# Attention with two feed-forward layers on one Trainium2 core: probabilities transposed in place for one more batch, a shared ring of five buffers, and deeper loads of 64-bit weights

## The chip, the core and the metric

The kernel runs on one core of a Trainium2 chip. The metric is the device time of one execution in microseconds (us). The core's engines are named as the profile names them: PE is TensorE's matmul, PEld its weight load, DVE is VectorE, ACT is ScalarE, POOL is GpSimd, and SP is SyncE, which here issues nearly all DMA transfers. Each engine takes the instructions of its own queue in order.

## The reference

Attention over 4 batches, 12 heads, 448 positions and 64 values per head, then two feed-forward layers, all in float32:

```python
def rmsnorm(x, g):
    rms = np.sqrt(np.mean(x * x, axis=-1, keepdims=True) + 1e-06)
    return x / rms * g
q_n, k_n = (rmsnorm(q, g_q), rmsnorm(k, g_k))
scores = scale * np.matmul(q_n, k_n.transpose(0, 1, 3, 2))
scores = scores - np.max(scores, axis=-1, keepdims=True)
attn = np.exp(scores)
attn = attn / (np.sum(attn, axis=-1, keepdims=True) + 1e-09)
...
return np.matmul(attn, v).astype(np.float32)
...
x = np.ascontiguousarray(attn_out.transpose(0, 2, 1, 3)).reshape(B * S, H * D)   # 1792 x 768
...
h = x @ w_in                    # first layer, 768 -> 2048
r = np.maximum(h, 0.0)
g = r * r
return (g @ w_out).astype(np.float32)
...
a = x @ w1                      # second layer, 768 -> 1024 -> 1024 -> 768
b = x @ w2
h = a * b @ w3
return (h @ w_out).astype(np.float32)
```

The weights reach the kernel as 64-bit floats; q, k, v and the result are float32.

## The kernel before, in words

**Precision.** A float32 operand is split into a high part, which the matmul's fp32r type holds, and the remaining low part. Each product is then three fp32r matmuls (lines L262, L263, L264 in `mm3`): high by high, high by low, low by high.

**Weights.** They come in units of 128 rows by 384 or 512 values. A 64-bit unit is loaded into a `raw64` tile (the trace calls it `raw`, L180, on SP's queue). ACT rewrites its upper words (L194), POOL or ACT its lower ones (L200, L198), and DVE joins the two into a float32 tile `raw` (L207). ACT copies that to the high half of `hl` (L106), and POOL or DVE subtracts to get the low half (L114). For the weights of the first feed-forward layer and of `w1` and `w2` the joined unit is also stored to DRAM (L215), so that later batches load 32-bit units (L183). The function `advance` keeps these steps ahead of the matmuls: when unit i is split, loads are issued up to unit i + `LOAD64_AHEAD`, words are rewritten up to i + 3 and joined up to i + 2. With 4 `raw64` buffers the load of unit i + 5 goes into the buffer of unit i + 1.

**The order of the work.** A loop runs over the 48 heads (12 for each batch). In the iteration of head h, PE computes the scores of head h in two halves (`stage_qk`), ACT takes the exponential of each half into a tile `p` (`stage_exp`, L543), and PE transposes the probabilities of head h - 1 (`stage_t`, L570: four blocks of 128 or 64 columns, four transposes each, so 16 for a head) and multiplies them by v (`stage_v`, L622). Between these steps `fill` puts feed-forward matmuls into PE's queue. While the heads of batch 1 run, the matmuls are those of w3 times w_out (`gen_w3o`, with 32 64-bit units); while the heads of batch 2 run, they are the feed-forward layers of batch 1 (`gen_moe(0)`, with 88 64-bit units and their stores); while those of batches 3 and 4 run, the layers of batches 2 and 3, from 32-bit units. The layers of batch 4 come last, without attention beside them. The framework fixes the order of each engine's queue when the program is built, from this program order and its own estimates of when things are ready; the trace shows, for example, transposes set between the two score matmuls of a head.

**Transposing probabilities.** In the first batch PE transposes the float32 tile `p` itself, against a float32 identity. From the second batch on (`h >= H`, H is 12) each half head's `p` is first copied by a DMA on SP's queue (L549, 392 KB) into a tile `pw`, which is declared as fp32r. PE then transposes `pw` against an fp32r identity. `p` and `pw` have 3 buffers each:

```python
pp = t3.tile([P, 2, S], F32, name="p", tag="p")
...
if h >= H:
    words = t3.tile([P, 2, S], F32R, name="pw", tag="pw")
    nc.sync.dma_start(out=words.bitcast(F32), in_=pp)
    d["p"][c0:c0 + 2] = [words[:, 0, :], words[:, 1, :]]
```

In `stage_t` the transposed block is rounded to its high half by ACT (L106, `ptr`) and its low half is made by DVE (L114, `ptr`), with two PSUM buffers `pt`.

Of the kernel before, what the change touches and what calls it, by code (L numbers as in the profile page):

```python
# [8 lines left out]
F32 = mybir.dt.float32  # L9
F32R = mybir.dt.float32r  # L10
U16 = mybir.dt.uint16
U32 = mybir.dt.uint32
# [17 lines left out]
def attention_moe_kernel(  # L30
# [16 lines left out]
    B, P, H, C, D = q_nat.shape  # L47
    S = P * C
# [26 lines left out]
    JOIN_AHEAD = 2  # L75
    WORD_AHEAD = 3
    LOAD32_AHEAD = 3
    LOAD64_AHEAD = 5

    const = ctx.enter_context(tc.tile_pool(name="const", bufs=1))  # L80
    xp = ctx.enter_context(tc.tile_pool(name="x", bufs=8))
# [7 lines left out]
    t3 = ctx.enter_context(tc.tile_pool(name="t3", bufs=3))  # L89
# [9 lines left out]
    ident = const.tile([P, P], F32, name="ident")  # L99
    ident_r = const.tile([P, P], F32R, name="ident_r")  # L100
# [3 lines left out]
    def copy_on(eng, out, in_):  # L104
        if eng == "a":
            nc.scalar.activation(out=out, in_=in_, func=AF.Copy)  # L106
        elif eng == "g":
            nc.gpsimd.tensor_scalar(out=out, in0=in_, scalar1=1.0, scalar2=1.0, op0=ALU.mult, op1=ALU.mult)
        else:
            nc.vector.tensor_copy(out=out, in_=in_)  # L110
# [60 lines left out]
    def is64(i):  # L171
        return units[i][0].dtype != F32

    def load_next():
        i = pos["load"]
        src = units[i][0]
        n = src.shape[-1]
        if is64(i):
            t = t3.tile([128, 512, 2], U32, name="raw64", tag="raw64", bufs=4)
            nc.sync.dma_start(out=t[:, :n, :], in_=src.bitcast(U32).rearrange("p (n t) -> p n t", t=2))  # L180
        else:
            t = rawp.tile([128, 512], F32, name="raw", tag="raw")
            nc.sync.dma_start(out=t[:, :n], in_=src)  # L183
        raws[i] = t
        pos["load"] += 1

    def load_to(i):
        while pos["load"] <= min(i, NU - 1) and is64(pos["load"]):
            load_next()
# [50 lines left out]
    def advance(u):  # L240
        while pos["lo"] <= min(u + SPLIT_AHEAD, NU - 1):
            i = pos["lo"]
            for k in range(pos["load"], min(i + LOAD64_AHEAD, NU - 1) + 1):
                if is64(k):
                    load_next()
                elif k <= i + LOAD32_AHEAD and (k <= pos["join"] or not is64(k - 1)):
                    load_next()
                else:
                    break
            upto("store", min(i + JOIN_AHEAD, pos["join"]) - 1, lambda k: is64(k) and store(k))  # L250
            upto("word", i + WORD_AHEAD, lambda k: is64(k) and words(k))
            upto("join", i + JOIN_AHEAD, lambda k: is64(k) and join(k))
            upto("hi", i + HI_AHEAD, split_hi)
            upto("lo", i, split_lo)
# [274 lines left out]
    def stage_exp(h, s):  # L529
        if not (0 <= h < NH):  # L530
            return
        d = heads[h]
        nb, o = d.pop("nb"), d.pop("sc")
        i = h % 2
        if s == 0 and i == 0:
            sums2[h // 2] = small.tile([P, 2, C], F32, name="sm", tag="sm")
        sm = sums2[h // 2]
        c0 = 2 * s
        pp = t3.tile([P, 2, S], F32, name="p", tag="p")
        for j in range(2):  # L540
            c = c0 + j
            p = d["p"][c] = pp[:, j, :]
            nc.scalar.activation(  # L543
                out=p, in_=o[j], func=AF.Exp, scale=d["rq"][:, c:c + 1], bias=nb[:, j:j + 1],
                accum_out=sm[:, i, c:c + 1],
            )
        if h >= H:
            words = t3.tile([P, 2, S], F32R, name="pw", tag="pw")
            nc.sync.dma_start(out=words.bitcast(F32), in_=pp)  # L549
            d["p"][c0:c0 + 2] = [words[:, 0, :], words[:, 1, :]]  # L550
        if s == 1 and i == 1:
            nc.vector.tensor_scalar(out=sm, in0=sm, scalar1=1e-9, scalar2=None, op0=ALU.add)
            rs = small.tile([P, 2, C], F32, name="rs", tag="rs")
            nc.vector.reciprocal(out=rs, in_=sm)
            wide = t1.tile([P, C, 2, D], F32, name="rsw", tag="rsw")
            nc.gpsimd.tensor_scalar(
                out=wide, in0=rs.rearrange("p i c -> p c i").unsqueeze(3).to_broadcast([P, C, 2, D]),
                scalar1=1.0, scalar2=1.0, op0=ALU.mult, op1=ALU.mult,
            )
            sums2[h // 2] = wide.rearrange("p c i d -> p c (i d)")  # L560

    def stage_t(h, kc):
        if not (0 <= h < NH):
            return
        d = heads[h]
        k0, kn = KCS[kc]
        ps = ps_pt.tile([128, 512], F32, name="pt", tag="pt")
        to, one = (ps.bitcast(F32R), ident_r) if h >= H else (ps, ident)
        for c in range(C):
            nc.tensor.transpose(to[:kn, c * P:(c + 1) * P], d["p"][c][:, k0:k0 + kn], one)  # L570
        if kn == 128:
            t = t3.tile([128, 2, S], F32R, name="ptr", tag="ptr", bufs=3)
            hi, lo = t[:, 0, :], t[:, 1, :]
            d["pt"][kc] = [hi, lo]
        else:
            t = t1.tile([128, S], F32R, name="pte", tag="pte")
            hi, lo = t[:kn, :], t[kn:, :]
            d["pt"][kc] = [t]
        copy_on("a", hi, ps[:kn, :S])
        d["lo"].append((lo, ps[:kn, :S], hi.bitcast(F32)))  # L580
# [95 lines left out]
    for h in range(NH + 1):  # L676
# [5 lines left out]
        stage_qk(h, 0)  # L682
        fill(n)
        stage_exp(h, 0)
        if h % H != 1:
            stage_x(h - 2)
        stage_t(h - 1, 0)
        stage_t(h - 1, 1)
        fill(n)
        stage_lo(h - 1)  # L690
        if h < NH:
            v_prep(h)
        fill(n)
        stage_k(h + 1)
        stage_t(h - 1, 2)
        stage_t(h - 1, 3)
        fill(n)
        stage_lo(h - 1)
        stage_qk(h, 1)
        fill(n)  # L700
        stage_exp(h, 1)
        fill(n)
        stage_v(h - 1)
# [64 lines left out]
```

## Time and profile before

| | us |
|---|---|
| median of three runs | 1239.81 |
| lowest, highest | 1237.89, 1242.05 |
| the profiled execution, its own time | 1239.56 |
| its span in the trace | 1237.8 |

The profiled execution is 0.25 us under the median. Its span is 1.76 us shorter than its own time; that remainder lies around the instructions. In the span the first exponential of head 12 (batch 2) starts at 183.4, that of head 24 at 475.0 and that of head 36 at 749.0. The last probability transposes are at 1019, and from about 1030 on only feed-forward matmuls run. A matmul's busy time overlaps that of its neighbour, so the distance between two starts, not the time of one, says how fast PE goes.

### The profile page before, as it was taken

How to read it: one execution, taken by the hardware profiler on the slowest of the kernel's cores; microseconds unless marked ns; L12 is line 12 of the kernel's file. 1: busy time of each engine (PE TensorE's matmuls, PEld its weight loads, DVE VectorE, ACT ScalarE, POOL GpSimd, SP SyncE). 2: the span in 40 equal slices, each digit the busy share in tenths (PEclk: the TensorE clock that was granted, in tenths of full speed). 3: DMA queues.
4: the chain of work that ended last, by engine and by line, in shares of the span. 5: the costliest groups of instructions: out<-in, count | busy, mean ns of one | idle time of the engine just before them, and what ended most of it. 6: DMA issues, size and time to landing. Idle time of an engine off the chain costs nothing.

```text
span 1237.8 us, 18914 instructions
## 1 busy us (share of the span) xinstructions
PE 1166.3 (94%) x6192; PEld 1054.4 (85%) x6192; DVE 710.7 (57%) x1314; ACT 727.7 (59%) x1553; POOL 784.9 (63%) x772
## 2 busy tenths in 40 slices
PE   3799999898898999999999999999999999999998
PEld 1588887787787888998998998999999999999998
DVE  6699888878888685546567555655664421012110
ACT  5888867667746655655645655656545554443342
POOL 5875434565776756765776664756766556678673
PEclk9899999999999999999999999999999999999999
DMA  6774547787888866455445455454444443433342
GB/s 214 242 227 131 159 140 218 254 272 249 280 259 257 257 192 194 132 155 147 148 127 154 140 155 161 143 154 121 141 138 120 135 136 112 113 109 105 105 120 93
DMA packets 111347, 207.63 MB, mean 168 GB/s; under 512 B 12208, under 2 KB 66704, under 8 KB 111248
## 3 DMA queue, kind: packets, MB, share of 16 engines
q1 hardware_dynamic: 107792, 200.92, 53.8%
q10 hardware_dynamic: 3456, 5.51, 1.2%
q8 instruction: 49, 0.80, 0.3%
q14 instruction: 50, 0.41, 0.1%
HBM read 149.95 MB, written 27.53 MB: 143 GB/s over the span
## 4 chain that ended last, share of the span: by engine, by line
PE 59%; DMA 4%; DVE 4%; ACT 2%; POOL 1%; issue 1%; ACTq 0%; SPq 0%; POOLq 0%; DVEq 0%
PE mm L262 17%; PE mm L264 17%; PE mm L263 17%; PE kv L622 3%; PE pt L570 2%; DMA pw<-p 2%; PE sc L525 1%; PE sc L524 1%; DMA raw<-w 1%; POOL hl L114 1%; ACT p L543 1%; DMA kn<-k_nat 1%; PE kv L508 1%; DVE nb L526 1%; DVE raw L207 0%
## 5 line engine op out<-in xcount | busy, mean ns | idle before, releaser
L114 POOL TENSOR_TENSOR hl<-raw,hl 128x384 fp32r<-128x384 f32 (+1 forms) x383 | 447.0, 1171 | 254.5 <-ACT hl L106 250.9
L106 ACT ACTIVATE hl<-raw 128x384 fp32r<-128x384 f32 (+1 forms) x416 | 233.8, 564 | 146.8 <-PE mm L264 82.0
L262 PE MATMUL mm<-x,hl 128*128 128x448 f32 (+1 forms) x832 | 311.3, 374 | 4.4 <-ACT x L106 1.8
L263 PE MATMUL mm<-x,hl 128*128 128x448 f32 (+1 forms) x832 | 307.2, 369 | 8.1 <-POOL x L114 8.1
L264 PE MATMUL mm<-x,hl 128*128 128x448 f32 (+1 forms) x832 | 306.4, 368 | 3.7 <-DVE hl L114 3.3
L262 PE MATMUL mm<-act,hl 128*128 128x448 f32 (+1 forms) x640 | 238.3, 372 | 0.0
L263 PE MATMUL mm<-act,hl 128*128 128x448 f32 (+1 forms) x640 | 235.7, 368 | 2.3 <-POOL act L114 2.3
L264 PE MATMUL mm<-act,hl 128*128 128x448 f32 (+1 forms) x640 | 235.0, 367 | 0.6 <-POOL hl L114 0.6
L543 ACT ACTIVATE p<-sc,nb,rr 112x448 f32<-112x448 f32 x192 | 137.4, 720 | 82.4 <-DVE nb L527 82.0
L263 PEld LDWEIGHTS mm<-x,hl 128*128 128x128 f32 x832 | 158.5, 190 | 21.9 <-POOL x L114 9.7
L262 PEld LDWEIGHTS mm<-x,hl 128*128 128x128 f32 x832 | 158.4, 190 | 19.6 <-ACT x L106 3.5
L264 PEld LDWEIGHTS mm<-x,hl 128*128 128x128 f32 x832 | 158.6, 191 | 18.3 <-DVE hl L114 4.0
L526 DVE TENSOR_REDUCE nb<-sc 112x1 f32<-112x448 f32 x192 | 113.2, 616 | 34.5 <-PE sc L525 33.0
L263 PEld LDWEIGHTS mm<-act,hl 128*128 128x128 f32 x640 | 122.0, 191 | 12.8 <-POOL act L114 3.6
L200 POOL TENSOR_SCALAR raw<-raw 128x384 uint32<-128x384 uint16 (+1 forms) x110 | 86.3, 785 | 73.3 <-DMA raw<-w_in 25.8
L264 PEld LDWEIGHTS mm<-act,hl 128*128 128x128 f32 x640 | 121.9, 190 | 10.9 <-POOL hl L114 1.3
L262 PEld LDWEIGHTS mm<-act,hl 128*128 128x128 f32 x640 | 122.2, 191 | 9.7 <-ACT act L106 0.2
L114 DVE TENSOR_TENSOR ptr<-pt,ptr 128x448 fp32r<-128x448 f32 x144 | 87.0, 619 | 71.7 <-ACT ptr L106 71.3
L207 DVE SCALAR_TENSOR_TENSOR raw<-raw 128x384 uint32<-128x384 uint32 (+1 forms) x120 | 86.8, 727 | 40.3 <-POOL hl L114 27.2
L114 POOL TENSOR_TENSOR act<-gf,act 128x448 fp32r<-128x448 f32 x80 | 97.8, 1223 | 9.5 <-ACT act L106 5.0
L194 ACT ACTIVATE raw<-raw 128x384 f32<-128x384 f32 (+1 forms) x120 | 70.7, 596 | 52.2 <-DMA raw<-w 19.6
L334 DVE TENSOR_TENSOR gf<-mm,r 128x448 f32<-128x448 f32 x64 | 39.8, 622 | 97.7 <-ACT r L330 97.3
(82 smaller groups left out, 1588.6 us busy)
## 6 DMA issues: line engine op xcount, KB each, us to landing
pw<-p SPq DMA_DIRECT2D x72, 392.0 KB, 4.2
raw<-f_in SPq DMA_DIRECT2D x96, 192.0 KB, 2.4
raw<-f_out SPq DMA_DIRECT2D x72, 256.0 KB, 2.7
raw<-f SPq DMA_DIRECT2D x96, 192.0 KB, 2.4
raw<-w_in SPq DMA_DIRECT2D x32, 384.0 KB, 4.4
raw<-w_out SPq DMA_DIRECT2D x24, 512.0 KB, 6.2
raw<-w SPq DMA_DIRECT2D x32, 384.0 KB, 4.9
raw<-w3o SPq DMA_DIRECT2D x48, 256.0 KB, 2.8
```

The costliest lines, as they stand in the source:

```text
L106: nc.scalar.activation(out=out, in_=in_, func=AF.Copy)
L114: e.tensor_tensor(out=out, in0=in0, in1=in1, op=ALU.subtract)
L194: nc.scalar.activation(out=hi, in_=hi, func=AF.Prelu, scale=2.0**-112, alpha=-(2.0**32))
L200: nc.gpsimd.tensor_scalar(out=t[:, :n, 0], in0=low, scalar1=2.0**-13, scalar2=2.0**-14 - 0.5, op0=ALU.mult, op1=ALU.add)
L207: nc.vector.scalar_tensor_tensor(out=f[:, :n].bitcast(U32), in0=t[:, :n, 1], scalar=3, in1=t[:, :n, 0], op0=ALU.logical_shift_left, op1=AL ...
L262: nc.tensor.matmul(ps, w[:, 0, wk, :], x[0], start=(i == 0), stop=False)
L263: nc.tensor.matmul(ps, w[:, 0, wk, :], x[1], start=False, stop=False)
L264: nc.tensor.matmul(ps, w[:, 1, wk, :], x[0], start=False, stop=(i == last))
L334: nc.vector.tensor_tensor(out=gf, in0=ps, in1=r, op=ALU.mult)
L526: nc.vector.tensor_reduce(out=nb[:, j:j + 1], in_=o[j], axis=AX.X, op=ALU.max, negate=True)
L543: nc.scalar.activation(out=p, in_=o[j], func=AF.Exp, scale=d["rq"][:, c:c + 1], bias=nb[:, j:j + 1], accum_out=sm[:, i, c:c + 1],)
L622: nc.tensor.matmul(ps[:, :S], w, m, start=(n == 0), stop=(n == len(ops) - 1))
```

## The change

Three numbers and two conditions change. The copy into `pw`, and the fp32r transpose that goes with it, begin with the third batch (`h >= 2 * H`) and no longer with the second; the second batch transposes float32 `p` as the first does. `p` and `pw` share one ring of five buffers where they had three each. The ring of `raw64` has six buffers and no longer four, and `LOAD64_AHEAD` is 7 and no longer 5, so the load of unit i + 7 goes into the buffer of unit i + 1.

```diff
-    LOAD64_AHEAD = 5
+    LOAD64_AHEAD = 7
...
         if is64(i):
-            t = t3.tile([128, 512, 2], U32, name="raw64", tag="raw64", bufs=4)
+            t = t3.tile([128, 512, 2], U32, name="raw64", tag="raw64", bufs=6)
...
-        pp = t3.tile([P, 2, S], F32, name="p", tag="p")
+        pp = t3.tile([P, 2, S], F32, name="p", tag="p", bufs=5)
...
-        if h >= H:
-            words = t3.tile([P, 2, S], F32R, name="pw", tag="pw")
+        if h >= 2 * H:
+            words = t3.tile([P, 2, S], F32R, name="pw", tag="p", bufs=5)
             nc.sync.dma_start(out=words.bitcast(F32), in_=pp)
             d["p"][c0:c0 + 2] = [words[:, 0, :], words[:, 1, :]]
...
-        to, one = (ps.bitcast(F32R), ident_r) if h >= H else (ps, ident)
+        to, one = (ps.bitcast(F32R), ident_r) if h >= 2 * H else (ps, ident)
```

## Rows read from the trace of the kernel before

**Rows 1.** Windows by stage: batch 1 from 70, batch 2, batch 3.

```profile
core 0: us, PE busy (x) PEld busy (x) DVE busy (x) ACT busy (x) POOL busy (x), PEclk, DMA share, GB/s
...
70.00:183.40 113.40, 104.25 (x637) 94.34 (x636) 99.16 (x210) 91.37 (x202) 56.68 (x74) 0.98 0.53 160
183.40:475.00 291.60, 264.30 (x1379) 235.29 (x1378) 237.59 (x427) 187.04 (x404) 178.94 (x187) 0.96 0.78 245
475.00:749.00 274.00, 271.06 (x1476) 246.83 (x1475) 159.75 (x286) 158.59 (x345) 183.49 (x170) 1.00 0.52 152
```

**Rows 2.** Waits of PE from 183.4 to 475: us in total, times, longest.

```profile
PE pt L570 <- DMA pw<-p: 11.1, 7, 2.6
PE sc L524 <- ACT p L543: 6.6, 6, 2.1
PE mm L264 <- DVE hl L114: 3.3, 2, 1.8
PE pt L570 <- DVE ptr L114: 1.9, 3, 1.0
PE mm L262 <- DVE gf L334: 1.6, 1, 1.6
PE mm L263 <- POOL x L114: 1.3, 1, 1.3
PE mm L611 <- DVE gf L334: 1.2, 1, 1.2
```

**Rows 3.** Waits of PE from 475 to 1030.

```profile
PE pt L570 <- DMA pw<-p: 2.4, 3, 1.0
```

**Rows 4.** Timeline of PE around 420, start and length; idle before in brackets.

```profile
420.28 0.28 PE L570 MATMUL pt<-ident_r,pw 112*128 112x112 f32 x2
423.11 0.81 PE L570 MATMUL pt<-ident_r,pw 112*128 112x112 f32 x6 [2.55 <-DMA pw<-p]
```

**Rows 5.** Windows of 8 us, first and last of six, columns as in Rows 1.

```profile
196.00:204.00 8.00, 6.65 (x29) 6.02 (x30) 5.11 (x10) 4.57 (x11) 3.79 (x5) 0.79 0.70 215
...
421.00:429.00 8.00, 5.89 (x25) 5.38 (x26) 5.08 (x10) 4.71 (x12) 3.18 (x5) 0.79 0.79 260
```

**Rows 6.** Timeline of PE in batch 1: eight float32 transposes, next matmul.

```profile
136.62 0.96 PE L570 MATMUL pt<-ident,p 112*128 112x112 f32 x8
137.35 0.42 PE L262 MATMUL mm<-act,hl 128*128 128x384 f32 x1
```

**Rows 7.** Timeline of PE in batch 3: fp32r transposes, and scores between.

```profile
597.68 0.73 PE L570 MATMUL pt<-ident_r,pw 112*128 112x112 f32 x8
598.25 0.44 PE L262 MATMUL mm<-x,hl 128*128 128x448 f32 x1
...
601.98 0.37 PE L525 MATMUL sc<-kt,ql 128*112 128x448 f32 x1
...
613.13 0.80 PE L570 MATMUL pt<-ident_r,pw 112*128 112x112 f32 x8
613.76 0.44 PE L262 MATMUL mm<-act,hl 128*128 128x448 f32 x1
```

**Rows 8.** Timeline of ACT in batch 3: the exponential of those scores.

```profile
604.33 0.71 ACT L543 ACTIVATE p<-sc,nb,rr 112x448 f32<-112x448 f32 x1
```

**Rows 9.** DMA issues: count, KB each, median us from issue to landing.

```profile
pw<-p SPq DMA_DIRECT2D x72, 392.0 KB, 4.2
```

**Rows 10.** Waits of the converting engines from 183.4 to 475, largest, smallest of six.

```profile
ACT raw L194 <- DMA raw<-w: 19.6, 11, 3.9
...
POOL raw L200 <- DMA raw<-w: 8.7, 7, 3.3
```

**Rows 11.** Waits of SP's queue from 183.4 to 475, the two largest.

```profile
SPq L180 <- DVE raw L207: 61.6, 35, 4.3
SPq L549 <- ACT ptr L106: 27.2, 7, 6.7
```

**Rows 12.** Waits from 15 to 75, the only one for a weight load.

```profile
POOL raw L200 <- DMA raw<-wo: 1.1, 1, 1.1
```

## The prediction

> **What bounds the kernel now.** I read the windows by stage first [rows 1]. In batch 3 PE is busy for 271.1 of 274.0 us at the full granted clock, and its only wait of note from batch 3 to the end of attention is 2.4 us for `pw` [rows 3]. From 475 on PE sets the time, and nothing that comes earlier there is worth anything. Batch 2 is different: PE is busy for 264.3 of 291.6 us, the clock is 0.96, DVE is at 81% and the DMA engines at 78%. The change acts here. Batch 1 lies between, with PE busy for 104.3 of 113.4 us after its start-up.
>
> Next I read what PE waits for in batch 2 [rows 2]. The list adds up to 27.0 us. The largest entry is the change's own subject: seven waits, 11.1 us, for the copy into `pw`. The other 15.9 us are waits for ACT, DVE and POOL.
>
> Then I read the clock. In batch 2 there are six stretches with a half-speed part in them; an 8 us window around each shows 0.79 (the first and the last of the six are in [rows 5]). In 8 us that is 8 x 0.21 = 1.7 us of lost PE time, about 10 us for six, which agrees with 0.04 x 291.6 = 11.7 by the rounded mean. Ahead of each, PE had stood still. In the last, it stood 2.55 us for `pw` after two transposes, and the slow stretch follows [rows 4]. Reading the timeline the same way, four of the six follow a wait for `pw` alone (at 197, 320, 399, 423), one a wait of 1.2 us for DVE and then one of 1.0 us for `pw` (243), and one a wait for ACT's exponential (365).
>
> **The change part by part, against the profiled execution (1239.56 us, 0.25 under the median).**
>
> *Copies removed in batch 2.* 24 copies of 392 KB, 4.2 us each from issue to landing [rows 9], leave SP's queue. The transposes then need only the exponential, which was finished before SP could issue the copy. Where PE waited 2.55 us, the copy takes longer than that, so the exponential had ended before PE arrived. Those seven waits fall away, with nothing right behind them that is late: −11.1 us [rows 2]. The bound on the other side is that half comes back a little later, because PE arrives earlier everywhere: −5.5.
>
> *Clock kept.* The four half-speed stretches that follow `pw` alone should go: 4 x 1.7 = −6.7 us [rows 5]. The bounds are two (−3.4) and all six (−10.1).
>
> *Float32 transposes in batch 2.* 12 heads have 16 transposes each, 24 sets of eight. A set of eight float32 transposes in batch 1 takes 137.35 − 136.62 = 0.73 us until the next matmul starts [rows 6]; a set of fp32r ones takes 0.57 or 0.63 [rows 7]. That is 0.10 to 0.16 a set, 2.4 to 3.8 us in all, on PE's path; I take +3.0. The Trainium skill, "FP8 and Floating Point Precision", section TensorE Precision Notes, says that true FP32 needs four passes through the array. By that rule the term would be some +41 us and the change would lose. The rows do not show it for transposes: their ratio is 0.73 / 0.63 to 0.73 / 0.57, 1.2 to 1.3.
>
> *Six `raw64` buffers, loads seven ahead.* ACT and POOL wait for weight loads in batch 2, six entries of 19.6 to 8.7 us and 78 us together [rows 10]. PE waits on none of it directly. What reaches PE is hidden in the 15.9 us of waits for ACT, DVE and POOL [rows 2]; that is the upper bound of this term, and nothing is the lower one. The load of unit i + 7 waits for the same join (unit i + 1) at the same place in SP's order as the load of unit i + 5 did, so SP stands as long as before at these loads (61.6 us) [rows 11]; the data just arrives two units earlier. In SP's queue each load passes two units' worth of stores and of q, k and v loads, but once: the rate of loads stays. Without the copies SP also stops standing for ACT (27.2 us in the largest entry) [rows 11], which held up every load behind it. Late weights should become rare. What does that give PE? The nearest row is batch 1 from 70 on: it has float32 transposes, no copies, the same converters and few late loads, and PE is still idle for 9.2 of 113.4 us, 8%, with DVE at 87% [rows 1]. Without `pw`, batch 2 is at 15.9 of 291.6, 5%, and DVE will rise from 81% to some 87% when the stage gets shorter. So I expect little, and take −3.
>
> *Start-up.* From 15 to 75 one converter waited 1.1 us for a weight load [rows 12]. Two earlier loads gain at most that, and cost what they delay behind them, about as little. I take 0.
>
> *The shared ring.* In batches 3 and 4 tiles go p, pw, p, pw through five buffers. A new `pw` takes the buffer of the `p` two half heads back, whose copy landed long before. A new `p` takes the buffer of the `pw` three half heads back. For the second half of head h that is the first half of head h - 1, read by transposes that stand ahead of head h's second score matmuls in PE's queue, and the exponential needs those scores anyway. The rows show the cover: transposes end at 597.68 + 0.73 = 598.41, the scores follow up to 601.98, the exponential starts at 604.33 [rows 7, 8], 5.9 us after the last reader. So 0; if the cover were gone, each 0.1 us in each of 48 half heads would cost 4.8 us, since PE has no idle time there.
>
> *Batches 3 and 4 and the tail.* Same PE work, no idle time to win: 0 [rows 1, 3].
>
> Sum: −11.1 − 6.7 + 3.0 − 3 = −17.8, so 1239.6 − 17.8 = 1221.8, forecast **1222 us**.
>
> **The rivals.**
>
> *A. The converters loosen too.* Late weights delay POOL and ACT, they delay DVE, and DVE holds PE. Half of the other waits goes (−8), and with them all six slow stretches (−10.1): −11.1 − 10.1 + 3.0 − 8 = −26.2, or 1213. For it: the 78 us of [rows 10], and the DMA engines at 78%, which lose 24 copies. Against it: batch 1's 8% with hardly any late load. If every wait of batch 2 went, 27.0 + 10.1 − 3.0 = 34 us, 1205 would be the floor.
>
> *B. The wait moves.* Batch 2 is near DVE's limit, and PE's waits for `pw` come back as waits for DVE or the exponential: half of the 11.1 remains, and only two slow stretches go. −5.5 − 3.4 + 3.0 = −5.9, or 1234. For it: DVE at 81% in batch 2, and the queues' new order, which the framework fixes when it builds. Against it: PE's waits for DVE in batch 2 are short (2 us at most) [rows 2].
>
> *C. Slower: the ring binds.* If the ring hands a new `p` a buffer whose reader is not as old as I worked out, an exponential stands for a transpose or for a copy of 4.2 us, and everything behind it on ACT stands too (`hl`, `ptr`, `kt`). A wait that reaches PE by 1 us in each of the 48 half heads costs 48 us: 1222 + 48 = 1270. It decides from 17.8 / 48 = 0.37 us a half head. For it: the margin is thin, since the copy already ends PE's wait three times in batches 3 and 4 [rows 3]. Against it: the 5.9 us of cover.
>
> *D. Slower: float32 goes through the array several times.* If a set of eight in heads 12 to 23 takes four times the 0.57 us of an fp32r set, 2.28 us, the term is 24 x 1.71 = +41 and not +3: 1222 + 38 = 1260. Against it stand the sets of batch 1, which lie between matmuls as well and take 0.73 [rows 6, 7]. This is the rule of the Trainium skill named above.
>
> *E. No gain.* The copy was only the last of several late things: PE would stand as long for the exponential, and the slow stretches stay. Then −3 to +3 remains: about 1240. Against it: in the seven waits the exponential had ended more than the length of PE's wait before.
>
> **How the numbers follow.** Forecast 0.48, A 0.22, B 0.16, E 0.06, C 0.05, D 0.01, and 0.02 for a gain under B's. The forecast's own range is 1216 to 1228. The range that should hold 8 in 10 takes in A down to near its floor and B: 1207 to 1236. About 0.3% (3.7 us) is what a measurement of this kernel can tell from no change: faster 0.87 (forecast, A, nearly all of B), same 0.06 (E's most, the small gains), slower 0.07 (C, D, a part of E).
>
> **What would show it.** Right: no wait of PE for `pw` before the heads of batch 3; batch 2, from head 12's first exponential to head 24's, at some 274 us and not 291.6; one or two half-speed stretches in it and not six; sets of float32 transposes at 0.73 us there; waits for weight loads of ACT and POOL far under 78 us; batches 3 and 4 as long as before. Wrong: PE waits for the exponential or for DVE that add up to over 20 us in batch 2 (B); exponentials in batches 3 and 4 that wait for a transpose or a copy (C); a batch 2 under 268 us (A).

## The result: slower by 0.9%, and the profile after

The changed kernel takes 1251.33 us (median of four runs, 1249.71 to 1252.56). The kernel before took 1240.93 beside it. The ratio is 1.0091 with an interval of 1.0071 to 1.0111. The forecast was 1222, and 1251 lies outside its range.

The profiled execution has a span of 1250.2 us. The first view is again the windows by stage, with the columns of [rows 1]: batch 1 from 70, batch 2, batch 3 of the changed kernel.

```profile
70.00:184.20 114.20, 106.85 (x636) 93.27 (x635) 99.05 (x208) 92.59 (x203) 56.35 (x75) 0.99 0.55 162
184.20:487.80 303.60, 272.11 (x1384) 237.41 (x1384) 238.84 (x426) 186.60 (x403) 172.92 (x185) 0.96 0.67 200
487.80:761.70 273.90, 270.30 (x1474) 246.69 (x1474) 161.48 (x285) 159.00 (x345) 182.96 (x170) 1.00 0.52 152
```

Batch 2 grew by 12.0 us, from 291.6 to 303.6 [rows 1]. Batch 3 has its old length to 0.1 us, and batch 1 is 0.8 longer. So nearly the whole loss arises where a gain of 17.8 was forecast. DVE, ACT and POOL have no more work there than before (busy for 238.8, 186.6 and 172.9 us against 237.6, 187.0 and 178.9), and the DMA engines moved 200 GB/s in place of 245 (24 copies of 392 KB are gone). PE's idle time grew by 4.2 us, from 27.3 to 31.5, and its busy time by 7.8, from 264.3 to 272.1. The float32 transposes and the longer half-speed stretches are in the busy time; a busy time is modelled and can cover a part of a wait.

The next view is the list of waits in batch 2 of the changed kernel: engine, line, what it waited for, us in total, times, longest. It answers to [rows 2, 10, 11].

```profile
PE sc L524 <- ACT p L543: 20.6, 12, 4.2
PE pt L570 <- DVE ptr L114: 5.1, 6, 2.3
PE mm L263 <- POOL x L114: 1.7, 1, 1.7
...
ACT raw L194 <- DMA raw<-w: 23.8, 16, 3.8
...
ACT raw L194 <- DMA raw<-w_out: 20.7, 13, 3.3
ACT raw L194 <- DMA raw<-w_in: 15.9, 11, 2.7
...
POOL raw L200 <- DMA raw<-w_in: 22.0, 12, 4.6
POOL raw L200 <- DMA raw<-w: 13.9, 16, 2.2
POOL raw L200 <- DMA raw<-w_out: 13.4, 11, 3.8
...
DVE raw L207 <- POOL hl L114: 43.7, 29, 4.5
...
SPq L180 <- DVE raw L207: 142.1, 62, 5.2
```

The wait for `pw` is gone, as it had to be. In its place PE's scores wait 20.6 us for exponentials, where they waited 6.6 [rows 2], and the transposes wait 5.1 for the low half of `ptr`, where they waited 1.9. The waits behind them grew as well, and these were to shrink. The six waits of ACT and POOL for weight loads add up to 109.7 us and not 78 [rows 10], although each load is issued two units further ahead. DVE's joins wait 43.7 us for POOL's low halves, and in the kernel before 25.5:

```profile
DVE raw L207 <- POOL hl L114: 25.5, 19, 2.5
```

SP stands 142.1 us at the loads and not 61.6 [rows 11].

How such a load wait reaches PE can be read from the timelines of the changed kernel at the start of batch 2 (ACT, DVE, PE). Each line has the start, the length, and in brackets the idle time before it and who ended that.

```profile
190.02 0.52 ACT L106 ACTIVATE hl<-raw 128x384 fp32r<-128x384 f32 x1
191.93 0.56 ACT L194 ACTIVATE raw<-raw 128x384 f32<-128x384 f32 x1 [1.39 <-DMA raw<-w_in]
192.38 0.70 ACT L543 ACTIVATE p<-sc,nb,rr 112x448 f32<-112x448 f32 x1
192.99 0.19 ACT L543 ACTIVATION_READ_ACCUMULATOR p<-sc,nb,rr 112x1 f32 x1
193.09 0.71 ACT L543 ACTIVATE p<-sc,nb,rr 112x448 f32<-112x448 f32 x1
...
191.47 0.15 DVE L527 TENSOR_TENSOR nb<-nb,rr 112x2 f32<-112x2 f32 x1
...
191.52 0.37 PE L262 MATMUL mm<-x,hl 128*128 128x448 f32 x1
193.23 0.45 PE L524 MATMUL sc<-kt,qh 128*112 128x448 f32 x1 [1.35 <-ACT p L543]
```

A rewrite of words (L194) stands in ACT's queue ahead of two exponentials. Its load lands late, and ACT stands 1.39 us. Not all of that is lost: the first exponential also needs DVE's `nb` (L527), which ended at 191.62. It starts at 192.38, so the rewrite puts it off by some 0.7 us. PE's next scores need the PSUM tile that the first exponential reads, and PE stands 1.35 us. In the kernel before, the same place looks like this on ACT, with PE's scores behind it:

```profile
188.48 0.52 ACT L106 ACTIVATE hl<-raw 128x384 fp32r<-128x384 f32 x1
190.13 0.72 ACT L543 ACTIVATE p<-sc,nb,rr 112x448 f32<-112x448 f32 x1 [1.12 <-DVE nb L527]
190.75 0.19 ACT L543 ACTIVATION_READ_ACCUMULATOR p<-sc,nb,rr 112x1 f32 x1
190.84 0.72 ACT L543 ACTIVATE p<-sc,nb,rr 112x448 f32<-112x448 f32 x1
191.45 0.20 ACT L543 ACTIVATION_READ_ACCUMULATOR p<-sc,nb,rr 112x1 f32 x1
191.67 0.54 ACT L106 ACTIVATE vt<-kv 64x448 f32<-64x448 f32 x1
192.23 0.56 ACT L194 ACTIVATE raw<-raw 128x384 f32<-128x384 f32 x1
...
190.99 0.46 PE L524 MATMUL sc<-kt,qh 128*112 128x448 f32 x1 [0.85 <-ACT p L543]
```

PE stands for the exponential here too, but 0.85 us and not 1.35. The rewrite comes after the exponentials and finds its data there. No line of the diff touches it. The framework, which fixes each queue when the program is built, has put it elsewhere.

Counted over the whole queues, with the conditions of the change alone (the first kernel below): of the 130 rewrites on ACT (L194 and L198), 39 stand earlier among ACT's other work (the splits into `hl` not counted) and 11 later; of the 110 rewrites L200 on POOL, 29 stand earlier and none later; DVE's joins move in both directions. PE's own order is the same but for the type of the transposes and two pairs of matmuls. With the whole change, 116 of the 130 rewrites on ACT stand earlier, by 9.4 instructions on average over units 40 to 119, most of those that batch 2 splits; with the conditions alone the same average is 2.0.

### The profile page after: what moved, and what is told of

It reads as the page before. It is cut to its first block, busy times and chain, and to the rows that moved or that the text cites. A ratio compares the mean times of both kernels' runs of the same rounds, so it can differ in the third digit from the quotient of the medians.

```text
span 1250.2 us, 18840 instructions
## 1 busy us (share of the span) xinstructions
PE 1176.5 (94%) x6192; PEld 1056.3 (84%) x6192; DVE 710.8 (57%) x1314; ACT 729.6 (58%) x1553; POOL 780.3 (62%) x772
## 4 chain that ended last, share of the span: by engine, by line
PE 60%; DVE 12%; DMA 11%; POOL 7%; ACT 5%; issue 4%; SPq 0%; POOLq 0%; DVEq 0%; ACTq 0%
PE mm L262 17%; PE mm L264 16%; PE mm L263 16%; POOL hl L114 3%; PE kv L622 3%; PE pt L570 3%; DVE raw L207 2%; DMA raw<-w 2%; DMA raw<-w_in 2%; DMA kn<-k_nat 2%; PE sc L524 2%; DVE nb L526 2%; PE sc L525 2%; DMA raw<-w_out 2%; ACT p L543 2%
## 5 line engine op out<-in xcount | busy, mean ns | idle before, releaser
L262 PEld LDWEIGHTS mm<-x,hl 128*128 128x128 f32 x832 | 158.5, 190 | 17.8 <-ACT x L106 2.5
L200 POOL TENSOR_SCALAR raw<-raw 128x384 uint32<-128x384 uint16 (+1 forms) x110 | 87.1, 792 | 89.2 <-DMA raw<-w_in 33.0
L264 PEld LDWEIGHTS mm<-act,hl 128*128 128x128 f32 x640 | 122.3, 191 | 11.6 <-POOL hl L114 2.2
L194 ACT ACTIVATE raw<-raw 128x384 f32<-128x384 f32 (+1 forms) x120 | 71.3, 600 | 69.0 <-DMA raw<-w 23.8
L524 PE MATMUL sc<-kt,qh 128*112 128x448 f32 x192 | 77.2, 402 | 30.6 <-ACT p L543 28.3
```

The source lines that it names most:

```text
L194: nc.scalar.activation(out=hi, in_=hi, func=AF.Prelu, scale=2.0**-112, alpha=-(2.0**32))
L200: nc.gpsimd.tensor_scalar(out=t[:, :n, 0], in0=low, scalar1=2.0**-13, scalar2=2.0**-14 - 0.5, op0=ALU.mult, op1=ALU.add)
L262: nc.tensor.matmul(ps, w[:, 0, wk, :], x[0], start=(i == 0), stop=False)
L264: nc.tensor.matmul(ps, w[:, 1, wk, :], x[0], start=False, stop=(i == last))
L524: nc.tensor.matmul(o[j], d["qh"][:, c * P:(c + 1) * P], d["kt"], start=True, stop=False)
```

## The experiments

The expectations name the theories by letters. **O**: the new order of the queues makes the loss, and the edits themselves would pay. **L**: the deeper loads make it. **R**: the shared ring makes it. **W** came later: in e11 and e12 it says that the four float32 `raw` tiles are too few, and the joins wait for them; in e5 to e8 the letter stands for a wider reading, told there. Other readings are told in the expectations too, and none of these letters is a rival of the prediction. Each kernel was timed in several rounds beside the kernel before on the same chip. "Batch 2" in the table is the distance between the first exponentials of heads 12 and 24 in the profiled execution, one for each kernel. That of e13 took 1243.3 us and that of e15 1249.0, 4.0 under and 3.1 over their medians, so these two lengths are off by about as much.

| run | median | ratio to before | batch 2 |
|---|---|---|---|
| before (first profile) | 1239.81 | | 291.6 |
| the change | 1251.33 | 1.0091 [1.0071, 1.0111] | 303.6 |
| e1_copies_only | 1248.93 | 1.0091 [1.0066, 1.0116] | 299.2 |
| e2_ring_only | 1237.68 | 0.9995 [0.9979, 1.0011] | 288.4 |
| e3_ring_loads | 1238.98 | 1.0008 [0.9994, 1.0022] | 293.9 |
| e4_copies_ring | 1248.46 | 1.0076 [1.0054, 1.0097] | 300.7 |
| e5_copies_held | 1238.27 | 0.9997 [0.9983, 1.0011] | 289.6 |
| e6_before_held | 1229.65 | 0.9937 [0.9918, 0.9956] | 283.7 |
| e7_copy_f32 | 1248.95 | 1.0088 [1.0070, 1.0107] | 300.8 |
| e8_nocopy_r | 1243.18 | 1.0036 [1.0016, 1.0055] | 295.7 |
| e9_copies_old_order | 1233.42 | 0.9963 [0.9946, 0.9980] | 284.4 |
| e10_before_new_order | 1267.53 | 1.0238 [1.0211, 1.0265] | 320.4 |
| e11_copies_raw6 | 1242.51 | 1.0037 [1.0020, 1.0053] | 293.1 |
| e12_before_raw6 | 1236.68 | 0.9982 [0.9967, 0.9997] | 285.9 |
| e13_old_order_act | 1247.34 | 1.0061 [1.0043, 1.0080] | 295.1 |
| e14_old_order_dve | 1244.48 | 1.0029 [1.0014, 1.0045] | 294.8 |
| e15_old_order_pool | 1245.84 | 1.0058 [1.0037, 1.0079] | 296.0 |
| e16_held_order | 1230.01 | 0.9920 [0.9893, 0.9948] | 281.9 |
| e17_after_old_order | 1228.86 | 0.9911 [0.9886, 0.9935] | 282.4 |
| e18_after_held_order | 1230.84 | 0.9926 [0.9896, 0.9955] | 284.2 |

### Which part makes the loss (e1 to e4)

The conditions alone, with the rings and loads of before:

```diff
-        if h >= H:
+        if h >= 2 * H:
...
-        to, one = (ps.bitcast(F32R), ident_r) if h >= H else (ps, ident)
+        to, one = (ps.bitcast(F32R), ident_r) if h >= 2 * H else (ps, ident)
```

> Only the two conditions change (copies from the third batch on); rings and loads stay as before. Theory L (the deeper 64-bit loads did the harm: ACT and POOL take up the words of a unit as soon as its load is due and stand for it, so exponentials come late): without them the copy's removal pays, batch 2 near 275 us, time about 1225 us. Theory C (the copies' removal did the harm: transposes and exponentials are queued closer together and PE stands for the exponential where it stood for the copy): PE waits for the exponential about 20 us in batch 2, time about 1250 us.

The shared ring alone, copies kept:

```diff
-        pp = t3.tile([P, 2, S], F32, name="p", tag="p")
+        pp = t3.tile([P, 2, S], F32, name="p", tag="p", bufs=5)
...
-            words = t3.tile([P, 2, S], F32R, name="pw", tag="pw")
+            words = t3.tile([P, 2, S], F32R, name="pw", tag="p", bufs=5)
```

> Only the ring changes: p and pw share five buffers, copies from the second batch on, loads as before. Theories L and C: no change, within 4 us of the kernel before. Theory R (the shared ring makes exponentials or copies wait, or reorders the queues): 1245 us or more, with waits of ACT for PE or a DMA at the exponential.

The ring and the loads, copies kept (on top of the diff of e2):

```diff
-    LOAD64_AHEAD = 5
+    LOAD64_AHEAD = 7
...
-            t = t3.tile([128, 512, 2], U32, name="raw64", tag="raw64", bufs=4)
+            t = t3.tile([128, 512, 2], U32, name="raw64", tag="raw64", bufs=6)
```

> The ring and the deeper loads (six buffers, seven ahead), with the copies still from the second batch on. Theory L: slower than before, about 1250 us or more, with ACT and POOL standing for weight loads some 120 us in batch 2 where it was 78. Theory C: no slower than before, 1235 to 1241 us.

The conditions and the ring, loads as before (the two diffs of e1 and e2 together):

> The copies' conditions and the ring, loads as before (four buffers, five ahead): the changed kernel without its loads. Theory L: about 1225 us, the change's gain laid bare. Theory C: about 1250 us, as the changed kernel.

The conditions alone lose as much as the whole change (1.0091 each). Ring and loads, alone and together, change nothing that can be measured, and the ring leaves the order of every queue as it was. Theories L and R fall, and of the theories of e1 to e4 C is left: its time was met, its wait for the exponential came to 15.0 us and not 20. The waits of PE in batch 2 of e1:

```profile
PE sc L524 <- ACT p L543: 15.0, 13, 2.6
PE pt L570 <- DVE ptr L114: 8.3, 11, 2.6
```

With the old buffers and the old load distance, PE waits for the same two engines as in the changed kernel. Two extra buffers for the loads gave no slack either: in e3 the six waits of ACT and POOL for loads add up to 87.9 us. Its rewrites stand 7.6 instructions earlier on ACT on average over units 40 to 119, so the two units of lead went into rewriting earlier. And yet e3 loses nothing, while e1, whose rewrites moved by 2.0, loses as much as the whole change. How far the rewrites move does not set the loss.

### What in the conditions costs (e5 to e8)

Holding each pair of rewrites of unit i, from the ninth of batch 2's units on, behind the high half of unit i - 3 on ACT and behind a low half of unit i - 4 or older on POOL, so that they can't move ahead. First with the conditions of e1, then on the kernel before:

```diff
+    def held(i):
+        with ExitStack() as s:
+            if i >= U0 + 8:
+                s.enter_context(tc.issue_after(hi_at[i - 3]))
+                s.enter_context(tc.issue_after(lo_at[max(k for k in lo_at if k <= i - 4)]))
+            words(i)
...
-            upto("word", i + WORD_AHEAD, lambda k: is64(k) and words(k))
+            upto("word", i + WORD_AHEAD, lambda k: is64(k) and held(k))
```

> No copies in batch 2 (as the run with the conditions alone, 1249 us), and the word rewrites of a 64-bit unit are held to their place in the program: on ACT behind the high half of the unit three before, on POOL behind a low half four or more before. Theory P (without the copies the framework's plan sets the rewrites earlier in the queues of ACT and POOL, where they stand for their loads with exponentials and ptr behind them): waits of ACT and POOL for weight loads in batch 2 fall from 105 us to under 60, and the time to 1225 to 1238 us. Theory F (the float32 transposes themselves) and theory W (batch 2 is held by the converters, and any wait removed comes back elsewhere): 1245 to 1252 us.

> The kernel before with the word rewrites held in the same way. Theory P: fewer waits for loads here too, 1225 to 1238 us. Theory W and F: within 4 us of the kernel before.

The copies kept in batch 2, but `pw` declared float32, so that the transposes are float32:

```diff
-            words = t3.tile([P, 2, S], F32R, name="pw", tag="pw")
+            words = t3.tile([P, 2, S], F32R if h >= 2 * H else F32, name="pw", tag="pw")
...
-        to, one = (ps.bitcast(F32R), ident_r) if h >= H else (ps, ident)
+        to, one = (ps.bitcast(F32R), ident_r) if h >= 2 * H else (ps, ident)
```

> The copies of batch 2 stay, but the copy is declared float32 and PE transposes it against the float32 identity there. Theory F: the float32 transposes cost what the change cost, about 1248 us. Theory P and W (the copies' absence does it): 1238 to 1243 us, the transposes' 3 us and no more.

The copies left out of batch 2, and the transposes still fp32r: the exponential writes `p` as fp32r there (which rounds the probabilities of batch 2):

```diff
-        pp = t3.tile([P, 2, S], F32, name="p", tag="p")
+        pp = t3.tile([P, 2, S], F32R if H <= h < 2 * H else F32, name="p", tag="p")
...
-        if h >= H:
+        if h >= 2 * H:
```

> No copies in batch 2, and ACT writes its probabilities there as fp32r, so that PE transposes them in fp32r without a copy; the probabilities of batch 2 are thereby rounded to fp32r. Theory F: with the float32 transposes gone the copies' removal pays, 1222 to 1235 us. Theory P and W: 1243 to 1250 us.

Holding the rewrites takes 10.7 us off e1 (1248.93 to 1238.27), and ACT's and POOL's waits for loads fall from 105.5 to 8.1 us. But it takes 8.5 off the kernel before as well, where 29.0 us of these waits are left. So the held plan is the better one for both kernels, and this pair doesn't show that the change made early rewrites dearer: between e6 and e5 the conditions still lose 8.6 us, and the two were planned apart as well.

e7 and e8 are the odd result. Either half of the conditions loses by itself: float32 transposes with the copies kept lose 10.8 us beside the kernel before, fp32r transposes without copies lose 5.0. If the parts had prices of their own, e8 should have gained. In e8, PE's scores wait 17.3 us for exponentials in batch 2, with no copy and no float32 transpose there. What e1, e7 and e8 share is that the queues were planned again. But e7 and e8 were not forced into an old order, so for them that cause is argued and not shown. In e7 PE's waits add up to 27.2 us, no more than the 27.0 of [rows 2]; it has the float32 transposes, and its half-speed stretches hold 27.3 us of batch 2 and not 20.5.

### The order by itself (e9, e10)

The kernel of e1, with the queues of all five engines forced into the order that the kernel before has (24 copies left out). At the end of the program, each instruction is made to follow its predecessor of that order, by a dependency that fixes the order and waits for nothing:

```diff
...
+    queues = {}
+    for ins in nc.cur_bb.bb.instructions:
+        queues.setdefault(str(ins.engine).split(".")[1], []).append(ins)
+    info = mybir.DependencyInfo(mybir.DependencyClass.NoSync, mybir.DependencyReason.DATA)
+    for e, order in PIN.items():
+        for a, b in zip(order, order[1:]):
+            tc.add_manual_dep(queues[e][b], queues[e][a].name, info, reason="order")
```

> The conditions alone (no copies and float32 transposes in batch 2, 1249 us so far), with the instructions of PE, ACT, DVE, POOL and SP forced into exactly the order that they have in the kernel before (the 24 copies left out). Theory O (the change lost by the new order that the framework gave the queues): the copies' waits are gone and nothing else has moved, 1222 to 1236 us. Theory X (it lost in execution, by what the engines do to one another without the copies and with longer transposes, in any order): 1244 to 1251 us.

And the reverse: the kernel before, copies and all, forced into the order of e1.

> The kernel before, copies and fp32r transposes and all, with its instructions forced into the order that they have in the kernel with the conditions alone; the copies stand where the framework puts them between. Theory O: slower than before, 1245 us or more. Theory X: within 4 us of the kernel before.

This decides for O against X, which looked for the loss in execution in any order. The same edit is 1248.93 in its own order and 1233.42 in the old one: the order costs 15.5 us, and the conditions by themselves gain 5.3 beside the kernel before (1238.72), 0.9963 with an interval that ends at 0.9980. The old kernel in the new order loses 28.8 us with no other edit; that order was made without the 24 copies, and PE waits 10.7 us for them there. No kernel was forced into its own order, but the forcing runs over the whole program, and outside batch 2 it costs nothing that can be seen: batch 1 from 70 on takes 113.5 us in e9 and 113.3 in e10 (before: 113.4), batch 3 takes 274.6 and 273.6 (before: 274.0). First batch 2 of e9, its window (columns as in [rows 1]) and its waits:

```profile
183.50:467.90 284.40, 262.90 (x1379) 231.74 (x1378) 239.85 (x426) 185.36 (x404) 180.93 (x187) 0.99 0.70 217
```

```profile
PE sc L524 <- ACT p L543: 7.1, 7, 2.4
PE pt L570 <- DVE ptr L114: 4.5, 6, 1.6
...
ACT raw L194 <- DMA raw<-w_in: 12.8, 8, 3.1
...
ACT raw L194 <- DMA raw<-w_out: 10.7, 4, 4.0
ACT raw L194 <- DMA raw<-w: 6.6, 6, 1.5
...
DVE raw L207 <- POOL hl L114: 23.3, 19, 2.4
```

Then batch 2 of e10, in the same two views:

```profile
183.30:503.70 320.40, 277.18 (x1387) 242.32 (x1386) 236.57 (x426) 187.49 (x405) 173.56 (x187) 0.94 0.73 222
```

```profile
PE sc L524 <- ACT p L543: 17.2, 13, 2.9
PE pt L570 <- DMA pw<-p: 10.7, 7, 4.0
PE pt L570 <- DVE ptr L114: 7.4, 8, 1.8
...
ACT raw L194 <- DMA raw<-w: 31.3, 17, 5.5
...
DVE raw L207 <- POOL hl L114: 49.0, 27, 4.9
```

The new order brings PE's wait for the exponential (17.2 us), ACT's waits for loads and DVE's for POOL (49.0) into the kernel before; the old order takes most of them out of e1, where they were 15.0 and 43.3 (7.1 and 23.3). The granted clock of batch 2 is 0.99 in e9 and 0.94 in e10.

### More float32 buffers (e11, e12)

Six `raw` tiles and not four, with the conditions of e1 and on the kernel before:

```diff
-    rawp = ctx.enter_context(tc.tile_pool(name="raw", bufs=4))
+    rawp = ctx.enter_context(tc.tile_pool(name="raw", bufs=6))
```

> The conditions alone, with six buffers for joined float32 units where there were four. There DVE stood 43 us in batch 2 at its joins for POOL, which frees those buffers (26 us in the kernel before). Theory W (DVE standing there makes exponentials and low halves late): that wait falls to under 15 us and the time to 1225 to 1240 us. Theory O or X without it: 1244 to 1251 us.

> The kernel before with six buffers for joined float32 units. Theory W: 1228 to 1236 us. Theory O or X: within 4 us of the kernel before.

They take 6.4 us off e1 and about 2.0 off the kernel before. W's own sign isn't there: DVE's joins still wait 41.1 us for POOL in e11, 43.3 in e1, where under 15 was expected. PE still waits 16.7 us for exponentials, and e11 stays slower than before. These kernels were planned again too, so the gain can't be put down to the buffers. In e12 77 of the 130 rewrites on ACT stand earlier than in the kernel before and none later, counted as above, and it is no slower: again the early rewrite alone is not the loss.

### One engine at a time, and the held order (e13 to e16)

The kernel of e1 with one engine's queue forced into the old order: ACT, DVE, POOL.

> The conditions alone (1249 us), with ACT's queue alone forced into the order of the kernel before (with all queues forced it was 1233 us). Theory A (word rewrites that moved ahead of exponentials on ACT stand for their loads): 1232 to 1238 us, and PE's waits for the exponential in batch 2 back near 9 us. Theory D (it is DVE's order) or P (POOL's): 1244 us or more.

> The same with DVE's queue alone forced into the old order. Theory D (joins and q work that moved ahead of reductions and low halves on DVE): 1232 to 1238 us. Theories A and P: 1244 us or more.

> The same with POOL's queue alone forced into the old order. Theory P (word rewrites that moved ahead of low halves on POOL hold back the joins on DVE): 1232 to 1238 us. Theories A and D: 1244 us or more.

The kernel of e1 with all queues in the order of e6:

> The conditions alone, with all queues forced into the order of the kernel before with its word rewrites held (1230 us). Theory O says that over one order the removal of the copies pays, by some 5 us over the old order: here 1222 to 1228 us, under both kernels and under the held kernel before. If the removal pays only where the copies' waits are 11 us (held they were about 3), it is 1228 to 1234 us.

By the medians ACT's order alone gives 1.6 us of the 15.5, DVE's 4.4, POOL's 3.1, which add up to 9.1. Each taken beside the kernel before that was timed with it, they are 2.6, 5.4 and 4.1, 12.1 of 15.7. None brings the time back to 1238, so the theories A, D and P of these runs, one engine alone, all fall. A's sign came without its gain: with ACT's order PE's wait for the exponential is back near its old size, and the time is not.

```profile
PE sc L524 <- ACT p L543: 9.2, 8, 2.7
```

The rest needs several queues to agree, or lies with SP's queue, which wasn't tried alone. So my picture of ACT's rewrites ahead of exponentials is at most one link. That the chain runs over DVE's joins and POOL's low halves too is read from their waits, and not shown.

e16 (1230.01) is no faster than e6 (1229.65), the same order with the copies. O had expected 1222 to 1228 here, and missed; the other reading held. Where the rewrites are held back, PE waits only 2.3 us for `pw` in batch 2 of e6, so little is left for the conditions to take away.

### The whole change in an old order (e17, e18)

The changed kernel with PE, ACT, DVE and POOL in the order of the kernel before (SP's queue free, since its loads are two units deeper), and the same with the order of e6:

> The changed kernel, whole, with the queues of PE, ACT, DVE and POOL forced into the order of the kernel before (SP's is left free). Theory O: the order alone made it slower; as the conditions alone in that order, or better by the late loads that are left: 1222 to 1234 us, with waits of ACT and POOL for weight loads in batch 2 under 30 us where the old order without the deeper loads has 59. If the deeper loads themselves do harm, over 1238 us.

> The changed kernel forced into the order of the kernel before with its word rewrites held (1230 us with and without copies). Theory O: 1224 to 1232 us, the best of both or equal to it; the deeper loads have little to give, since the held rewrites wait little for loads.

e17 beats both kernels: 1228.86, 0.9911 with an interval of 0.9886 to 0.9935. The change is worth about −10.8 us in the old order and loses 10.4 in its own, each beside the kernel before (1239.67 and 1240.93). In the order of e6 it is worth nothing: e18 takes 1230.84, and e6 itself 1229.65. So −10.8 is its worth in the old order, not in every order. Batch 2 of e17, window and waits:

```profile
182.40:464.80 282.40, 265.12 (x1381) 234.38 (x1380) 239.80 (x426) 183.37 (x404) 178.59 (x187) 0.98 0.71 216
```

```profile
PE sc L524 <- ACT p L543: 6.5, 6, 2.4
PE mm L264 <- DVE hl L114: 3.1, 3, 1.8
PE pt L570 <- DVE ptr L114: 1.6, 5, 0.5
...
ACT p L543 <- DVE nb L527: 66.4, 20, 8.7
...
SPq L180 <- DVE raw L207: 109.5, 58, 5.3
```

No rewrite of ACT or POOL waits for a load any more: 0 us, where the kernel before has 78 [rows 10] and the changed kernel 109.7. With the rewrites kept at their places, two more units of lead do become slack. PE's list is close to that of [rows 2] without `pw` (16.8 us in all, and 15.9 there). ACT now stands 66.4 us for DVE's row maxima, and PE doesn't mind: this is idle time of an engine that isn't late.

## Why the prediction was wrong, point by point

**The copies, −11.1: this step failed.** "Those seven waits fall away, with nothing right behind them that is late" was read from the queues as they stood. In the changed kernel PE's waits for the exponential and for `ptr` rose from 8.5 to 25.7 us, more than the 11.1 that went. In the old order the step holds in part. In e9, the conditions alone, PE's waits in batch 2 add up to 20.9 us where they were 27.0 [rows 2]: 11.1 went and 5.0 came back, near the half that stood as the bound on the other side. By the medians e9 gains 5.3 us, and the three terms of the prediction for the conditions (−11.1, −6.7, +3.0) come to −14.8, so they were too large even with the queues unmoved. With the deeper loads, in e17, the two waits are 8.1 us and all of PE's 16.8. I had taken the queues as fixed and read the gain from one wait in them. The edit that removes the wait also re-planned all of them.

**The clock, −6.7: wrong in the changed kernel, right in e9, half right in e17.** I forecast one or two half-speed stretches in batch 2. There are five, 23.9 us together, where the kernel before has six with 20.5 us. Four of the five begin where PE stands, or has just stood, 1.5 to 3.0 us for an exponential or for `ptr`; ahead of the one at 374.8 the trace shows no wait in 7 us. So they come with other waits as well as with `pw`, and the sum in the prediction tied them to `pw` alone. e9 has two with 6.8 us (−6.6 in the table below), e17 three with 13.7 (−3.7), e10 nine with 41.0.

**Float32 transposes, +3.0: right.** A set of eight takes 0.70 us until the next matmul starts, in batch 2 of the changed kernel:

```profile
382.94 0.93 PE L570 MATMUL pt<-ident,p 112*128 112x112 f32 x8
383.64 0.45 PE L262 MATMUL mm<-act,hl 128*128 128x448 f32 x1
```

That is 0.07 to 0.13 more than an fp32r set [rows 7], 1.7 to 3.1 us in 24 sets. The four passes of rival D don't show. The Trainium skill, "Perfetto Trace Analysis", section Transposes, says that a transpose skips the arithmetic by logic of its own, and the 0.70 us of the row agree.

**The loads, −3, and "late weights should become rare": failed, by the same omission.** The load was to arrive two units earlier, before a rewrite that stays where it is. The planner moved the rewrites earlier instead, and the waits rose from 78 to 109.7 us. That SP stands as long as before at these loads was not right either: it stood 61.6 us there before and 142.1 after. Much of that comes with the missing copies, at which SP no longer stands: e9, with the old loads and the old order, has 106.7. In e17 SP still stands 109.5, and late weights are gone all the same. From e9 to e17 (ring, deeper loads, SP's queue free) the gain beside the kernel before grows from 5.3 to 10.8 us, so the term −3 is too small there, if SP's order has no part in it; the two profiled executions differ by less, 1231.51 and 1229.66.

**The shared ring, 0, and start-up, 0: right.** e2 is 0.9995. Head 12's first exponential comes 0.8 us later than before, at 184.2. No exponential of batches 3 and 4 held PE up; from 487.8 to the end of attention the list begins as [rows 3] did:

```profile
PE pt L570 <- DMA pw<-p: 2.8, 3, 1.2
```

**Batches 3 and 4, 0: right** (273.9 us for batch 3, 274.0 before).

**The rivals.** B came nearest. Its mechanism, the wait moving to the exponential and to DVE, is what the trace shows, and its sign, "over 20 us in batch 2", was met. I had named "the queues' new order" there as a doubt, and still priced B as half of one wait, a gain of 5.9, when a new order has no bound in the rows of the old one. E, "no gain", and C, the ring, didn't happen. A slower case that rests on the order was missing, though it was as open as the faster one; with it the range could not have ended at 1236.

**How the 12 us come about.** The distances between the starts of PE's matmuls in batch 2 (from head 12's first score to head 24's, with the same counts of each kind) can be sorted into work and standing: what exceeds the usual distance of that kind, twice that at half speed, is put to the releaser that the profile names. These sums are a little above those of the waits view, since a modelled busy time overlaps the gap. They depend on which distance is taken as usual, and are good to some 2 us.

| us | before | changed | e9 | e17 | e10 |
|---|---|---|---|---|---|
| batch 2 on PE | 285.2 | 297.8 | 278.1 | 275.9 | 313.8 |
| standing for exponentials | 8.3 | 24.5 | 9.3 | 8.3 | 20.6 |
| standing for `pw` | 12.4 | 0 | 0 | 0 | 12.0 |
| standing for DVE's `ptr` | 2.8 | 6.4 | 6.1 | 2.9 | 9.0 |
| in transposes | 15.4 | 18.4 | 17.3 | 17.3 | 16.3 |
| lost to half speed | 9.9 | 11.6 | 3.3 | 6.2 | 19.5 |

From before to changed: +16.2 − 12.4 + 3.6 + 3.0 + 1.7 = +12.1 of the 12.6. The half-speed part of a transpose is in two rows, a small double count. From before to e17: 0 − 12.4 + 0.1 + 1.9 − 3.7 = −14.1, and the batch is 9.3 shorter; the difference of 4.8 lies in rows that I didn't sort further. Of the 17.8 us forecast, the old order delivers 10.8.

**What stays open.** Why the planner moves the rewrites when a copy goes or a type changes: its estimates weren't examined, only their outcome. Which part of the new order makes the loss: how far the rewrites move doesn't follow the times (e3, e12). How the 15.5 us of e1 divide among the queues beyond the 9.1 to 12.1 that single engines gave, and what SP's queue alone does. And why batch 2 with its rewrites held (e6, 283.7 us) and without copies in the old order (e17, 282.4) end at about the same length; PE is idle for about 17 to 20 us of it in both.

## What to carry to other kernels

Where a framework plans the queues when it builds, an edit that removes a transfer or changes a type is two edits: the one in the diff, and a new order of every queue. Compare the order of the queues before costing anything, and force the old order on the changed program to learn what the diff is worth there; here that was −10.8 us against +10.4, and about 0 in a third order. A deeper prefetch gives slack only if its consumer stays where it was: the same two buffers brought the waits for loads to 0 in one order and to 109.7 us in another.

## What the runs showed that I had not expected

The order of the queues alone, with the same instructions, moves this kernel by 2.4% (e10, 1.0238), more than any part of the change does in either direction. Each half of the conditions by itself, a float32 type with the copies (e7) and no copies with fp32r (e8), made the kernel slower, by 10.8 and 5.0 us. And one constraint on the rewrites, for which PE never waits directly, made the kernel before 0.6% faster (e6, 0.9937); its queues were planned again with it.
